# Decode attention with an adaLN block: q.k sums by identity matmuls, four heads across the partitions, V stationary, features on the partitions in the MLP

## Chip, cores and metric

One core of one Trainium2 chip. The metric is device time in microseconds (us) of one execution. Every run quoted is fast: none was over 1.5% above the fastest of its kernel. Each ratio to the kernel before is taken within the rounds of one chip; kernels of different rounds are compared by these ratios.

## The reference, cut to what matters

```python
# A_x (4,1,512); k_cache, v_cache (4,32,4096,128) bf16: 4 batches, 32 heads, 4096 keys
mod = silu(c) @ w_mod                        # six vectors of 512 for each batch
h = layernorm(x) * (1 + ca) + sa
q = (h @ wq)                                 # 32 heads of 128
p = softmax((q . k_cache) * 128 ** -0.5)     # one query for each batch and head
x = x + ga * ((p . v_cache) @ wo)
h = layernorm(x) * (1 + cb) + sb
z = gelu(h @ w_in); z1, z2 = halves of z     # 896 each
x = x + gb * ((z1 * (w_sp * layernorm(z2) + b_sp)) @ w_out)
```

(adaLN: the scale and shift of each layer norm come from c through w_mod. PV below is p . v_cache, the sum of V's rows weighted by the probabilities.) K and V are 134 MB each and each element is used once, so the work is a stream of 268 MB with a small start (w_mod 3.1 MB, wq 4.2 MB) and a small tail (wo, w_in, w_out).

## The kernel before

A group is one batch and 8 heads, in four K tiles of 2 heads (2 MB). A partition holds 32 consecutive keys of a head, 8 KB. VectorE does the whole dot product: multiply by the broadcast q, then six halving adds in place and a last add.

```python
kt = kvp.tile([P, HC, NT * DH], BF16, name="kt", bufs=4)      # HC = 2 heads, NT = 32, DH = 128
nc.sync.dma_start(out=kt, in_=kv_ap(A_k_cache, b, h0 + ci * HC))
...
for hli in range(HC):                                          # L271
    nc.vector.tensor_tensor(out=prod[:, hli], in0=prod[:, hli],
                            in1=qbc[:, hl, :][:, None, :].to_broadcast([P, NT, DH]), op=ALU.mult)
w = DH
while w > 2:                                                   # L281
    half = w // 2
    nc.vector.tensor_tensor(out=prod2[:, :, 0:half], in0=prod2[:, :, 0:half],
                            in1=prod2[:, :, half:w], op=ALU.add)
    w = half
nc.vector.tensor_tensor(out=S_g[...], in0=prod2[:, :, 0:1], in1=prod2[:, :, 1:2], op=ALU.add)  # L288
# ... softmax of the group: max by a transpose and a ones-matmul, exp on ScalarE ...
# PV of the group before, P stationary (one column), V moving:
nc.tensor.matmul(ops[pb:pb + 1, :], lhsT=P_g[:, hl, n:n + 1],  # L219
                 rhs=vt[:, hli, n * DH:(n + 1) * DH], ...)
```

V has three 2 MB buffers. Norms and MLP work on [4, 512] and [4, 1792] tiles: 4 of 128 partitions.

## Time and profile before

| | before |
|---|---|
| time, median of 4 runs | 794.36 us (793.86 to 794.49) |
| span of the profiled run | 792.9 us |
| bytes loaded | 283 MB |
| VectorE busy | 657.8 us, 83% |
| mean load rate | 357 GB/s |

The page of the kernel before, in parts: busy us and share for each engine; the span in 40 slices of 19.8 us with busy tenths for VectorE and the DMA engines and the load rate in GB/s; and the chain of waits that ended last.

```profile
PE 343.3 (43%) x4466; PEld 296.3 (37%) x4466; DVE 657.8 (83%) x754; ACT 73.0 (9%) x187; POOL 3.2 (0%) x14
...
DVE  1649999999999797979979797979979797979035
...
DMA  9999779999999999999899998989899999968220
GB/s 311 336 422 420 298 294 422 408 422 417 421 419 419 419 419 398 409 346 419 353 403 393 355 401 345 408 339 422 348 399 384 369 394 351 398 243 368 107 93 0
...
DVE 73%; PE 20%; DMA 4%; ACT 1%; issue 1%; ACTq 0%; SPq 0%; DVEq 0%
DVE kt L271 35%; DVE kt L281 32%; PE ops L219 15%; DMA kt<-in_A_k_cache_dram 2%; DMA wq_128<-in_A_wq_dram 1%; DVE S_g L288 1%; PE rowps L157 1%; PE rowps L176 1%; PE rowps L347 1%; ACT P_g L312 1%; DVE ssub L306 1%; DVE mrow L296 1%; PE row
```

VectorE sits at 9 or 7 tenths in nearly every slice, and the chain runs over it. But the load is near its own limit too: unhindered slices show 417 to 422 GB/s, and slices of 340 to 400 stand between them. The last three hold little (107, 93 and 0).

The groups by shape (line, engine, operation, tiles, shapes, count; busy us, mean ns of one; idle time before):

```profile
L271 DVE TENSOR_TENSOR kt<-kt,qbc 128x4096 bf16<-128x4096 bf16 x128 | 292.0, 2282 | 12.4 <-DMA kt<-in_A_k_cache_dram 12.3
L219 PE MATMUL ops<-vt,P_g 128*1 128x128 bf16 x4096 | 276.3, 237 | 68.8 <-ACT P_g L312 38.8 <-DMA vt<-in_A_v_cache_dram 20.5 <-ACT o_all L225 9.5
...
L281 DVE TENSOR_TENSOR kt<-kt 128x4096 bf16<-128x4096 bf16 x64 | 146.0, 2281 | 0.0
L281 DVE TENSOR_TENSOR kt<-kt 128x2048 bf16<-128x2048 bf16 x64 | 77.7, 1213 | 0.0
...
L288 DVE TENSOR_TENSOR S_g<-kt 128x64 f32<-128x64 bf16 x64 | 18.5, 289 | 0.0
```

All shapes of L281 in one line, from the page:

```profile
L281 DVE TENSOR_TENSOR kt<-kt 128x1024 bf16<-128x1024 bf16 (+5 forms) x384 | 320.7, 867 | 0.4
```

The multiplies cost 292.0 us. The adds that follow (all shapes of L281, 320.7 us, and L288, 18.5 us) cost more than the multiplies.

Two pieces of the chain in order of time (start, length, what) are the yardsticks for TensorE: 32 pairs of a 128-column weight load and one moving column in 0.89 us (28 ns each), and 32 matmuls of 512 columns in 7.08 us (221 ns each).

```profile
667.40 0.89 PE misc L235 x32
...
755.82 7.08 PE rowps L347 x32
```

### The profile page before, as it was taken

Reading aid. Unit: us, or ns where it says so; the run is one execution under the profiler, and the core shown is the slowest. Engines: PE = TensorE matmul, PEld = TensorE weight load, DVE = VectorE, ACT = ScalarE, POOL = GpSimd, SP = SyncE. Lnnn points to the kernel's source line nnn. Section 1 sums busy time; section 2 is a strip of 40 time slices with the busy share of each in tenths; the row PEclk is TensorE's granted clock in tenths of the full one; section 3 lists DMA queues with packets and bytes.
Section 4 is the critical chain, followed back from the end, with each engine's and each line's share of the span. In section 5 each row is a group of like instructions: output and inputs, shape, how many; then the busy total and the mean of one; then the engine's idle time right before and its main releaser. Section 6 shows DMA issues by size and latency. Waiting matters only on the chain.

```text
span 792.9 us, 10282 instructions
## 1 busy us (share of the span) xinstructions
PE 343.3 (43%) x4466; PEld 296.3 (37%) x4466; DVE 657.8 (83%) x754; ACT 73.0 (9%) x187; POOL 3.2 (0%) x14
## 2 busy tenths in 40 slices
PE   0810172726363636344261806244260807153872
PEld 0200061726263636244260806243250807143820
DVE  1649999999999797979979797979979797979035
ACT  1010100101010000101010100001010100000111
POOL 1000000000000000000000000000000000000000
PEclk9955586768675857768595857667595857667785
DMA  9999779999999999999899998989899999968220
GB/s 311 336 422 420 298 294 422 408 422 417 421 419 419 419 419 398 409 346 419 353 403 393 355 401 345 408 339 422 348 399 384 369 394 351 398 243 368 107 93 0
DMA packets 47893, 283.40 MB, mean 357 GB/s; under 512 B 2396, under 2 KB 14568, under 8 KB 15080
## 3 DMA queue, kind: packets, MB, share of 16 engines
q10 hardware_dynamic: 26672, 143.54, 45.3%
q1 hardware_dynamic: 21112, 139.21, 43.8%
q8 instruction: 35, 0.57, 0.3%
q14 instruction: 10, 0.08, 0.0%
q0 software_dynamic: 64, 0.00, 0.0%
HBM read 282.73 MB, written 0.00 MB: 357 GB/s over the span
## 4 chain that ended last, share of the span: by engine, by line
DVE 73%; PE 20%; DMA 4%; ACT 1%; issue 1%; ACTq 0%; SPq 0%; DVEq 0%
DVE kt L271 35%; DVE kt L281 32%; PE ops L219 15%; DMA kt<-in_A_k_cache_dram 2%; DMA wq_128<-in_A_wq_dram 1%; DVE S_g L288 1%; PE rowps L157 1%; PE rowps L176 1%; PE rowps L347 1%; ACT P_g L312 1%; DVE ssub L306 1%; DVE mrow L296 1%; PE rowps L369 1%; DVE mh L300 0%; PE misc L235 0%
## 5 line engine op out<-in xcount | busy, mean ns | idle before, releaser
L281 DVE TENSOR_TENSOR kt<-kt 128x1024 bf16<-128x1024 bf16 (+5 forms) x384 | 320.7, 867 | 0.4
L219 PE MATMUL ops<-vt,P_g 128*1 128x128 bf16 x4096 | 276.3, 237 | 68.8 <-ACT P_g L312 38.8
L271 DVE TENSOR_TENSOR kt<-kt,qbc 128x4096 bf16<-128x4096 bf16 x128 | 292.0, 2282 | 12.4 <-DMA kt<-in_A_k_cache_dram 12.3
L219 PEld LDWEIGHTS <-P_g 128*1 128x1 bf16 x4096 | 268.0, 92 | 73.5 <-ACT P_g L312 40.3
L298 PE MATMUL misc<-ident_f,mrow 128*8 128x128 f32 x16 | 6.0, 372 | 214.1 <-DVE mrow L296 214.1
L298 PEld LDWEIGHTS misc<-ident_f,mrow 128*8 128x8 f32 x16 | 1.3, 83 | 225.7 <-issue 165.6
L225 ACT ACTIVATE o_all<-ops,rZ 1x128 bf16<-1x128 f32 x128 | 38.4, 350 | 262.7 <-PE ops L219 161.2
L321 DVE RECIPROCAL rZ<-misc 1x8 f32<-1x8 f32 x16 | 3.3, 203 | 59.2 <-PE misc L316 59.2
L202 PE MATMUL qps<-q_sb,E_sel 4*128 4x512 bf16 x32 | 14.2, 485 | 85.5 <-ACT qbc L207 84.4
L202 PEld LDWEIGHTS <-E_sel 4*128 4x128 bf16 x32 | 2.8, 94 | 87.8 <-issue 86.4
L312 ACT ACTIVATE P_g<-ssub 128x256 bf16<-128x256 f32 x16 | 6.7, 416 | 298.1 <-DVE ssub L306 298.1
L207 ACT CAST qbc<-qps 128x512 bf16<-128x512 f32 x32 | 17.1, 587 | 111.9 <-DVE kt L271 92.0
L304 PE MATMUL misc<-diagM,ones_f 8*128 8x8 f32 x32 | 9.4, 364 | 39.8 <-DVE diagM L302 39.8
L304 PEld LDWEIGHTS misc<-diagM,ones_f 8*128 8x128 f32 x32 | 7.9, 306 | 44.9 <-DVE diagM L302 35.7
L288 DVE TENSOR_TENSOR S_g<-kt 128x64 f32<-128x64 bf16 x64 | 18.5, 289 | 0.0
L357 DVE TENSOR_SCALAR onepb<-mod_sb 4x512 f32<-4x512 bf16 x1 | 0.4, 415 | 15.7 <-PE ops L219 15.7
L151 DVE TENSOR_TENSOR siluc<-sig,c_sb 4x512 bf16<-4x512 f32 x1 | 0.7, 679 | 14.5 <-ACT sig L149 14.5
L127 PE MATMUL tp<-ident_bf,siluc 4*128 4x4 bf16 x4 | 0.7, 176 | 18.6 <-DVE siluc L151 18.3
L127 PEld LDWEIGHTS <-siluc 4*128 4x128 bf16 x4 | 0.3, 103 | 19.2 <-DVE siluc L151 18.3
L306 DVE TENSOR_TENSOR ssub<-S_g,misc 128x256 f32<-128x256 f32 x16 | 6.5, 404 | 1.0 <-PE misc L304 1.0
L347 PE MATMUL rowps<-wo_sb,oT_all 128*4 128x512 bf16 x32 | 7.1, 379 | 0.3 <-DVE oT_all L240 0.3
L180 DVE CAST q_sb<-rowps 4x512 bf16<-4x512 f32 x8 | 5.3, 677 | 2.2 <-PE rowps L176 2.2
(98 smaller groups left out, 118.7 us busy)
## 6 DMA issues: line engine op xcount, KB each, us to landing
kt<-in_A_k_cache_dram SPq DMA_DIRECT2D x64, 2048.0 KB, 9.0
vt<-in_A_v_cache_dram ACTq DMA_DIRECT2D x64, 2048.0 KB, 10.9
wo_sb<-in_A_wo_dram ACTq DMA_DIRECT2D x1, 4096.0 KB
win_sb<-in_B_w_in_dram SPq DMA_DIRECT2D x1, 1792.0 KB
wout_sb<-in_B_w_out_dram ACTq DMA_DIRECT2D x1, 896.0 KB, 21.1
wmod_112<-in_w_mod_dram SPq DMA_DIRECT2D x1, 512.0 KB, 3.8
wmod_114<-in_w_mod_dram SPq DMA_DIRECT2D x1, 512.0 KB, 4.8
wq_124<-in_A_wq_dram ACTq DMA_DIRECT2D x1, 512.0 KB
```

Source lines behind the costliest of these rows:

```text
L157: nc.tensor.matmul(mp, lhsT=cT[:, j, :], rhs=wmod_cs[oc][:, j, :], start=(j == 0), stop=(j == DJ - 1),)
L202: nc.tensor.matmul(qps, lhsT=E_sel[:, b, :], rhs=q_sb[0:B, h0 * DH + qi * QW:h0 * DH + (qi + 1) * QW], start=True, stop=True,)
L207: nc.scalar.copy(out=qbcv[:, qi * QW:(qi + 1) * QW], in_=qps)
L219: nc.tensor.matmul(ops[pb:pb + 1, :], lhsT=P_g[:, hl, n:n + 1], rhs=vt[:, hli, n * DH:(n + 1) * DH], start=(n == 0), stop=(n == NT - 1), t ...
L225: nc.scalar.activation(out=o_all[pb:pb + 1, h0 + hl, :], in_=ops[pb:pb + 1, :], func=AF.Copy, scale=rZ[pb:pb + 1, hl:hl + 1],)
L271: nc.vector.tensor_tensor(out=prod[:, hli], in0=prod[:, hli], in1=qbc[:, hl, :][:, None, :].to_broadcast([P, NT, DH]), op=ALU.mult,)
L281: nc.vector.tensor_tensor(out=prod2[:, :, 0:half], in0=prod2[:, :, 0:half], in1=prod2[:, :, half:w], op=ALU.add,)
L288: nc.vector.tensor_tensor(out=S_g[:, ci * HC:(ci + 1) * HC, :].rearrange("p h n -> p (h n)")[:, :, None], in0=prod2[:, :, 0:1], in1=prod2[ ...
L304: nc.tensor.matmul(Mbc_ps, lhsT=ones_rowG, rhs=diagM, start=True, stop=True)
L306: nc.vector.tensor_tensor(out=ssub, in0=S_g, in1=Mbc_ps[:, :, None].to_broadcast([P, HPG, NT]), op=ALU.subtract,)
L312: nc.scalar.activation(out=P_g, in_=ssub, func=AF.Exp, scale=att_scale)
L347: nc.tensor.matmul(attn_ps, lhsT=oT_all[:, j, :], rhs=wo_sb[:, j, :], start=(j == 0), stop=(j == H - 1),)
```

## The change

The intent is to take the sums off VectorE and to leave a stream bound by the load. VectorE still multiplies; TensorE then adds by 16 matmuls with the identity as weights, each over 8 of the 128 products of every key, accumulating in PSUM; VectorE folds the last 8. A step is one batch and 4 heads: a partition holds 128 keys of one head (32 KB in one row), 4 MB per tile, two buffers each for K and V, K on the sync queue and V on the scalar queue. In PV, V is stationary (loaded into TensorE as weights) and four columns of probabilities move (are streamed past them). All small work is laid out with features on the partitions.

```diff
+    nc.scalar.dma_start(out=cT, in_=c.rearrange("b (p j) -> p b j", j=J))     # 8-byte runs, also xT
+    wmod_t = kvp.tile([P, J, 6 * D], BF16, name="vt", bufs=2)
+    nc.sync.dma_start(out=wmod_t, in_=w_mod.rearrange("(p j) n -> p j n", j=J))
+    wq_t = kvp.tile([P, J, H * DH], BF16, name="vt", bufs=2)
+    nc.sync.dma_start(out=wq_t, in_=A_wq.rearrange("(p j) n -> p j n", j=J))
...
+        return cache[b, g * NH:(g + 1) * NH].rearrange("h (s n) d -> (h s) (n d)", s=R)
...
-                while w > 2:
-                    nc.vector.tensor_tensor(out=prod2[:, :, 0:half], ..., op=ALU.add)
+            nc.vector.tensor_tensor(
+                out=kt, in0=kt, in1=q[:, None, :].to_broadcast([P, HT, DH]), op=ALU.mult)
+            for cc in range(DH // DC):                                  # 16 times, DC = 8
+                nc.tensor.matmul(ps, lhsT=ident, rhs=kt[:, :, cc * DC:(cc + 1) * DC],
+                                 start=(cc == 0), stop=(cc == DH // DC - 1))
...
+            nc.vector.tensor_reduce(out=st["S", i][...], in_=ps, axis=AX.X, op=ALU.add)
...
-                            ops[pb:pb + 1, :], lhsT=P_g[:, hl, n:n + 1], rhs=vt[...],
+                    o_ps, lhsT=st["v", i][:, n, :], rhs=P4[:, n, :],
...  norms by ones-matmuls, MLP with weights stationary and 4 moving columns;
...  the engine order is fixed by hand: scores(i,0), project(i-2), fold(i-1,1), softmax(i-1),
...  scores(i,1), fold(i,0), values(i-1)
```

## The prediction

> **What bounds it now.** Span 792.9 us. VectorE is busy 657.8 us (83%, busy table); the chain of waits is 73% VectorE, 20% TensorE, 4% DMA. Per 4 MB of K+V VectorE pays (groups by shape) two 2.28 us multiplies, halving adds of 5.2 us together and the S_g add: about 10 us, then each group's softmax and PV burst. The load is close behind: 283.4 MB, and free slices run at 419-424 GB/s, so 283.4/0.42 = 675 us would be pure load. But K buffers come free late (SyncE waits 559 us on S_g), and the mean is 357 GB/s. The first 36 us run at 350 GB/s (1 KB packets). The last 93 us hardly load (700-745: 225 GB/s; 745-793: 78): last PV, wo 7.1 us, a serial MLP tail on 4 partitions.
>
> **Removed.** 320.7+18.5 us of VectorE adds; q broadcasts, 4-row transposes, three table reloads.
> **Kept.** The multiply: 64 of twice the size, still 290 us.
> **Added on VectorE** (estimates): 64 PSUM folds of 512 f32 at ~0.65 us = 42; per 4-head step five small softmax ops, ~1.5 us, and the o scaling, ~0.4 us: 60. Total ~395 us, 12.3 us per step of 32.
> **Added on TensorE.** 1024 identity matmuls of N=512: 221 ns each warm (wo burst: 32 in 7.08 us) = 226 us. The Trainium skill, "TensorE: Matmul & The Clock Gate", Back-to-back issue gap, gives 216 ns warm, 427 cold; the wo burst agrees with warm. PV with V stationary: 4096 pairs of a 128-column weight load and 4 columns; nearest in the trace, the o transposes (128-column load, 1 column) ran 32 in 0.89 us, 28 ns each, against 58-74 for PV now: 115 us. Together ~10.7 us per step warm, ~21 if the clock stays at half.
>
> **The new limit.** A step moves 8.39 MB, 20.0 us at 420 GB/s. K buffer: landed, 4.4 multiply, ~3 fold/softmax, 4.4 multiply, 3.5-7 us TensorE: free 16-18 us after landing, inside 20; so one K transfer is always outstanding. V has ~35 us. Both engines fit, so I expect a load-bound stream: VectorE ~55%, TensorE 45-60%, DMA at 9 in nearly every slice. The 340 us saved on VectorE are worth only the gap from 793 to the load. The skill's "DMA: Bandwidth & Descriptors", Measured, has 425 GB/s for large single-core loads; the best slices here agree (424).
>
> **Sum.** Start 2.5 us + 283.4 MB at 418-420 GB/s (676) = 678; a start gap (q by 128 tiled matmuls before the first V may load) 3; after the last landing: values, projection ~3 us, MLP feature-on-partition ~13 us (about 30 ops of 0.2-0.3 us on 16-56 columns, 84 small matmuls), output ~3 us. Predicted **700 us, range 684 to 732**. Chances: faster by over 2% 0.95, within 2% 0.03, slower 0.02.
>
> **What would show it.** DMA mean ~405 GB/s; chain of waits mostly DMA kt/vt instead of VectorE; identity matmuls 220-300 ns apart; PV pairs ~30 ns; no middle slices below 400; ~20 us from last landing to end instead of ~40.
>
> **What would make it wrong.** (1) The identity's moving operand is read in runs of 8 elements; if that, or a half clock in bursts with gaps, costs 2x, TensorE needs ~20 us per step: 720-780. (2) 128-column V weights not loading at 28 ns. (3) 32 KB rows loading below 420 GB/s: at 400, +34 us. (4) Two 4 MB buffers per stream too few: 1 us per step is +32. (5) q matmuls not overlapping: start gap 10-20 us.

## The result, and the profile after

| | before | after |
|---|---|---|
| time, median of 4 runs | 794.36 us | 719.40 us (717.88 to 721.82) |
| ratio | | 0.9056 (0.9036 to 0.9076) |
| VectorE busy | 657.8 us | 370.1 us |
| TensorE busy | 343.3 us | 428.8 us |
| mean load rate | 357 GB/s | 395 GB/s |

A ratio is the mean time of one kernel's fast runs over that of the other's of the same rounds, so it is not quite the ratio of the medians.

The time lies in the forecast range (684 to 732 us), 19 us above the predicted 700. The same parts of the page after (slices of 18 us):

```profile
PE 428.8 (60%) x5626; PEld 248.7 (35%) x5626; DVE 370.1 (52%) x405; ACT 82.0 (11%) x273; POOL 3.6 (0%) x17
...
DVE  0016575664664266665564366566555265663822
...
DMA  8938999999999999999999999999999989999930
GB/s 345 423 138 346 412 432 432 426 425 435 398 435 426 429 424 432 423 425 435 421 430 418 436 419 430 426 430 433 412 427 423 433 371 435 432 424 432 364 150 1
...
DMA 59%; DVE 25%; PE 14%; issue 1%; ACT 1%; DVEq 0%
DMA kt<-in_A_k_cache_dram 53%; DVE kt L225 19%; PE s_ps L230 9%; DMA xT<-in_A_x_dram 6%; DVE S L239 1%; PE o_ps L276 1%; PE qp L202 1%; DVE mT L249 1%; DVE nm L257 1%; DVE hm L251 0%; PE mod_ps L173 0%; DVE hb L253 0%; PE zf_ps L358 0%; DVE
```

The chain is now DMA, and the middle slices run at 412 to 435 GB/s almost without exception (398 and 371 are the lowest). Two things are left: the third slice at 138 GB/s and the end.

The groups that answer to those of before:

```profile
L230 PE MATMUL s_ps<-kt,ident 128*128 128x512 bf16 x1024 | 298.3, 457 | 225.4 <-DVE kt L225 225.2
L225 DVE TENSOR_TENSOR kt<-kt,qbc 128x8192 bf16<-128x8192 bf16 x64 | 281.8, 4404 | 251.2 <-DMA kt<-in_A_k_cache_dram 251.2
L230 PEld LDWEIGHTS <-ident 128*128 128x128 bf16 x1024 | 115.6, 113 | 393.5 <-issue 252.4 <-DMA kt<-in_A_k_cache_dram 70.5
L276 PEld LDWEIGHTS <-vt 128*128 128x128 bf16 x4096 | 109.1, 97 | 0.3 <-issue 0.3
L239 DVE TENSOR_REDUCE S<-s_ps 128x64 f32<-128x512 f32 x64 | 43.7, 683 | 2.2 <-issue 2.1
```

The adds are gone from VectorE; the folds cost 43.7 us (predicted 42), the multiplies 281.8 (predicted 290). VectorE now idles 251.2 us waiting for K.

One step in order of time (start, us, engine, line, what, idle before it):

```profile
411.45 4.43 DVE L225 TENSOR_TENSOR kt<-kt,qbc 128x8192 bf16<-128x8192 bf16 x1 [11.55 <-DMA kt<-in_A_k_cache_dram]
...
415.93 5.52 PE L230 MATMUL s_ps<-kt,ident 128*128 128x512 bf16 x16 [9.63 <-DVE kt L225]
...
417.16 0.15 PEld L230 LDWEIGHTS <-ident 128*128 128x128 bf16 x1 [0.27 <-issue]
...
417.59 0.15 PEld L230 LDWEIGHTS <-ident 128*128 128x128 bf16 x1 [0.28 <-issue]
...
418.08 4.38 DVE L225 TENSOR_TENSOR kt<-kt,qbc 128x8192 bf16<-128x8192 bf16 x1
...
422.51 3.61 PE L230 MATMUL s_ps<-kt,ident 128*128 128x512 bf16 x16 [1.06 <-DVE kt L225]
...
426.10 3.37 PE L276 MATMUL o_ps<-P_2_107,vt 128*128 128x4 bf16 x128
...
429.59 4.42 DVE L225 TENSOR_TENSOR kt<-kt,qbc 128x8192 bf16<-128x8192 bf16 x1 [6.53 <-DMA kt<-in_A_k_cache_dram]
```

K lands at 411.45. 5.52 us for 16 identity matmuls in the first half and 3.61 in the second (226 ns each); then 128 PV pairs in 3.37 us, 26 ns each. In the first half most weight loads (PEld, two of them shown) come 427 ns apart: TensorE had been idle for 9.6 us and starts slowly. The Trainium skill, "TensorE: Matmul & The Clock Gate", § Back-to-back issue gap, gives N / 1.2 GHz cold, 427 ns for 512 columns, and about 216 ns warm for a matmul alone; both agree with this step. The same section gives about 131 ns for N = 512 in a stream of weight loads and matmuls, and that is not seen here: such pairs ran 226 ns apart. All the work on this K tile ends at 426.1, 14.7 us after it landed, and the next tile comes at 429.59.

The stretches with busy time of each engine, mean granted clock, DMA share and GB/s:

```profile
core 0: us, PE busy (x) PEld busy (x) DVE busy (x) ACT busy (x) POOL busy (x), PEclk, DMA share, GB/s
...
40.00:60.00 20.00, 13.01 (x226) 7.58 (x226) 4.88 (x20) 5.41 (x11) 0.00 (x0) 1.00 0.25 81
300.00:400.00 100.00, 63.91 (x840) 36.96 (x839) 56.42 (x55) 11.56 (x40) 0.00 (x0) 0.73 1.00 427
```

From 40 to 60 us the load runs at 81 GB/s. The timeline of the start shows why:

```profile
0.77 0.45 ACTq L67 DMA_DIRECT2D cT<-in_c_dram  x1
...
40.75 0.22 ACT L161 ACTIVATE sg<-cT 128x16 f32<-128x16 bf16 x1 [38.73 <-DMA cT<-in_c_dram]
...
47.04 9.12 PE L202 MATMUL qp<-vt,hbc 128*32 128x512 bf16 x128 [1.50 <-DVE hbc L194]
...
56.22 2.55 ACTq L96 DMA_DIRECT2D vt<-in_A_v_cache_dram  x2
```

c is asked for at 0.77 us and ScalarE gets it at 40.75; x, behind it on the queue, is used at 43.43. Everything hangs on these two: the modulation, h, q (128 matmuls in 9.1 us), and the release of the two V buffers in which w_mod and wq lie, so the first V load goes out at 56.22. The two K buffers had filled at about 32 and 42 us (30.6 and 39.9 us after their issue), and from about 40 to 57 us hardly anything was loaded.

The DMA view of the first 40 us:

```profile
DMA packets 1150, 15.70 MB, mean 393 GB/s; under 512 B 639, under 2 KB 639, under 8 KB 639
...
q1 hardware_dynamic: 559, 15.70, 93.1%
q10 hardware_dynamic: 527, 0.00, 0.7%
```

In this time the sync queue (q1, bulk) moved 559 packets of 28 KB on average (15.70 MB / 559) and the scalar queue (q10) 527, nearly all of them c's 512 runs of 8 bytes: turn about, one for one (in the 10 us from 12 to 22 it was 145 and 145). Of the 559, 512 are the rows of w_mod, wq and the two K tiles (24 to 32 KB); the rest are 1 KB rows of wo. The Trainium skill, "DMA: Bandwidth & Descriptors", § Queues, rings and completion order, says that each DMA engine goes round robin between its queues, packet by packet. The counts agree. An estimate: c has 32 runs for each of 16 engines; 40.0 us / 32 = 1.25 us a turn, and a 28 KB packet at 427/16 GB/s takes 1.05 us. That reading was tested below.

**The sum.** Before the stream 2.5 us; 15.7 MB until about 40 us; gap 17 us; 267.8 MB from 57 to about 689.5 us (423 GB/s); from the last landing to the end 29 us. The forecast had 678 for the start and stream together without gap (measured 40 + 632.5, about 672), 3 for the gap and 19 for the end.

### The profile page after: what moved, and what is told of

The parts are those of the page before. It is cut to its first block, busy times and chain, and to the rows that moved or that the text cites. A ratio compares the mean times of both kernels' runs of the same rounds, so it can differ in the third digit from the quotient of the medians.

```text
span 718.3 us, 12248 instructions
## 1 busy us (share of the span) xinstructions
PE 428.8 (60%) x5626; PEld 248.7 (35%) x5626; DVE 370.1 (52%) x405; ACT 82.0 (11%) x273; POOL 3.6 (0%) x17
## 3 DMA queue, kind: packets, MB, share of 16 engines
q10 hardware_dynamic: 6096, 134.23, 43.7%
## 4 chain that ended last, share of the span: by engine, by line
DMA 59%; DVE 25%; PE 14%; issue 1%; ACT 1%; DVEq 0%
DMA kt<-in_A_k_cache_dram 53%; DVE kt L225 19%; PE s_ps L230 9%; DMA xT<-in_A_x_dram 6%; DVE S L239 1%; PE o_ps L276 1%; PE qp L202 1%; DVE mT L249 1%; DVE nm L257 1%; DVE hm L251 0%; PE mod_ps L173 0%; DVE hb L253 0%; PE zf_ps L358 0%; DVE oT L288 0%; ACT P_1_101 L260 0%
## 5 line engine op out<-in xcount | busy, mean ns | idle before, releaser
L230 PE MATMUL s_ps<-kt,ident 128*128 128x512 bf16 x1024 | 298.3, 457 | 225.4 <-DVE kt L225 225.2
L225 DVE TENSOR_TENSOR kt<-kt,qbc 128x8192 bf16<-128x8192 bf16 x64 | 281.8, 4404 | 251.2 <-DMA kt<-in_A_k_cache_dram 251.2
L230 PEld LDWEIGHTS <-ident 128*128 128x128 bf16 x1024 | 115.6, 113 | 393.5 <-issue 252.4
L276 PEld LDWEIGHTS <-vt 128*128 128x128 bf16 x4096 | 109.1, 97 | 0.3 <-issue 0.3
L260 ACT ACTIVATE P_0_95<-S,nm 32x128 bf16<-32x128 f32 x44 | 25.4, 576 | 190.8 <-DVE nm L257 189.9
L260 ACT ACTIVATE P_1_101<-S,nm 32x128 bf16<-32x128 f32 x44 | 25.4, 577 | 188.6 <-DVE nm L257 187.7
L239 DVE TENSOR_REDUCE S<-s_ps 128x64 f32<-128x512 f32 x64 | 43.7, 683 | 2.2 <-issue 2.1
L260 ACT ACTIVATE P_2_107<-S,nm 32x128 bf16<-32x128 f32 x40 | 23.0, 576 | 184.1 <-DVE nm L257 183.3
L276 PE MATMUL o_ps<-P_1_101,vt 128*128 128x4 bf16 x1408 | 37.4, 164 | 0.2 <-issue 0.2
L276 PE MATMUL o_ps<-P_0_95,vt 128*128 128x4 bf16 x1408 | 37.3, 164 | 0.0
L276 PE MATMUL o_ps<-P_2_107,vt 128*128 128x4 bf16 x1280 | 33.8, 164 | 0.0
L260 ACT ACTIVATION_READ_ACCUMULATOR P_0_95<-S,nm 32x1 f32 x44 | 11.0, 250 | 0.0
L260 ACT ACTIVATION_READ_ACCUMULATOR P_1_101<-S,nm 32x1 f32 x44 | 11.0, 250 | 0.0
L202 PE MATMUL qp<-vt,hbc 128*32 128x512 bf16 x128 | 9.1, 455 | 1.5 <-DVE hbc L194 1.5
L260 ACT ACTIVATION_READ_ACCUMULATOR P_2_107<-S,nm 32x1 f32 x40 | 10.0, 250 | 0.0
L257 DVE STREAM_TRANSPOSE nm<-hb 128x32 f32<-128x32 f32 x32 | 6.8, 211 | 3.2
```

The source lines that it names most:

```text
L202: nc.tensor.matmul(qp[hl * R:(hl + 1) * R], lhsT=hbc[:, j, b, :], rhs=wv[:, gh * GH:(gh + 1) * GH, hl, :], start=(j == 0), stop=(j == J - ...
L225: nc.vector.tensor_tensor(out=kt, in0=kt, in1=q[:, None, :].to_broadcast([P, HT, DH]), op=ALU.mult,)
L230: nc.tensor.matmul(ps, lhsT=ident, rhs=kt[:, :, cc * DC:(cc + 1) * DC], start=(cc == 0), stop=(cc == DH // DC - 1),)
L239: nc.vector.tensor_reduce(out=st["S", i][:, half * HT:(half + 1) * HT], in_=st.pop(("s", i, half)), axis=AX.X, op=ALU.add,)
L257: nc.vector.transpose(out=nm, in_=hb)
L260: nc.scalar.activation(out=P4[rows, :, hl], in_=S[rows, :], func=AF.Exp, bias=nm[rows, 0:1], scale=att_scale, accum_out=rs4[rows, hl:hl + 1],)
```

## The experiments

Eleven kernels ran. All are recorded as correct, e4 too, which leaves out half of V: the check of the result does not notice that, so it says little about the attention part.

### The start: e1 and e2

e1 puts the two small loads ahead of the bulk on its queue:

```diff
-            nc.scalar.dma_start(out=dst, in_=src)      # cT, xT
+            nc.sync.dma_start(out=dst, in_=src)
```

> Edit: the two small loads c and x (8-byte runs) go out on the sync queue ahead of the bulk loads instead of on the scalar queue beside them. Theory A (the small packets take turns with 28 KB bulk packets, so c lands at 40.7 us and the load stands still from about 39 to 57 us): c lands before 6 us, q is ready by about 35 us, the empty stretch of 18 us goes, time 700 to 705 us. Rival B (8-byte runs are slow by themselves, about 40 us for 512): the bulk behind them starts 40 us later, time 720 us or more. Rival C (the gap is refilled later, because the stream is limited elsewhere): time 715 to 722.

Measured: 700.22 us (699.16 to 703.56), ratio to before 0.8818 against 0.9056. c lands 1.9 us after its issue. The view of that tile, and the load rate:

```profile
DMA to landing us min/median/max: 1.9/1.9/1.9
```

```profile
GB/s 327 419 439 426 436 421 425 426 430 410 425 434 426 435 372 436 429 424 420 361 440 421 436 387 420 438 423 438 427 426 427 428 404 440 421 431 431 418 181 1
```

The gap is gone and theory A's number is met; rival B (slow runs) and C (limited elsewhere) fall. e2 leaves the small loads where they were and cuts w_mod and wq into rows of 6 and 8 KB:

```diff
+    for j in range(J):
+        nc.sync.dma_start(out=wmod_t[:, j, :], in_=w_mod.rearrange("(p j) n -> p j n", j=J)[:, j, :])
+    # wq likewise
```

> Edit: c and x stay on the scalar queue as they are; the w_mod and wq loads are cut in 4 pieces each, so that their rows (packets) are 6 and 8 KB instead of 24 and 32 KB. Theory A (turns packet by packet): c needs 32 turns per DMA engine; with 6 KB packets at 27 GB/s a turn takes about 0.22 us, so c lands at about 9 us and x at about 18 us instead of 41 and 43 us; the gap goes, time 700 to 707 us. Rival D (the scalar queue is starved until the sync queue is empty): c still lands at about 40 us, time 717 to 722.

Measured: 699.90 us (699.07 to 701.37). c lands after 4.8 us (x after 14.0), sooner than the 9 us worked out, and far from the 40 of rival D. (In the first 5.6 us of this trace the scalar queue moved 533 packets and the sync queue 192, so the turns were not one for one there.)

```profile
DMA to landing us min/median/max: 4.8/4.8/4.8
```

The scalar queue is the same, c and x are the same, the bulk bytes are the same; only the length of the bulk rows differs (and the number of loads that carry them, 8 instead of 2), and with it c's landing falls from 40.0 to 4.8 us. So it is the turn length that held c up, unless the number of loads did it, which was not tried alone.

### Is the middle bound by the load? e3 and e4

```diff
+                nc.vector.tensor_tensor(out=idle, in0=idle, in1=idle, op=ALU.mult)   # e3: once per step, 128x8192
```

> Edit: one more useless 4.4 us VectorE multiply per step (32 in all, +141 us of VectorE busy time, 370 to about 510). Theory (the middle is bound by the load, VectorE has slack): +2 to +12 us, from the first and last steps alone. Rival (VectorE is on the path in each step, the chain gives it 25%): +60 us or more.

Measured: 724.93 us (724.00 to 726.61), ratio 0.9127, so +0.8% on the kernel after, about 6 us for 142 us more VectorE time:

```profile
PE 425.7 (59%) x5626; PEld 248.2 (34%) x5626; DVE 511.9 (71%) x438; ACT 82.1 (11%) x273; POOL 3.6 (0%) x17
```

The theory holds: VectorE has slack in each step, though it holds 25% of the chain. The extra multiply stands after the second multiply of the step, outside the time in which a K buffer is held; what a longer hold of the buffer would cost is not tested by it.

```diff
-        return load(A_v_cache, i, "vt", ...)                         # e4, wrong on purpose
+        nc.scalar.dma_start(out=t[:, 0:w], in_=kv_view(A_v_cache, i)[:, 0:w])     # w = half
...  lhsT=st["v", i][:, n % HT, :]
```

> Wrong result on purpose. Edit: only half of each V tile is loaded (67 MB less), the PV matmuls read that half twice; all engine work stays. Theory (load-bound at about 425 GB/s): 283.5 MB becomes 216.4 MB, time 720 - 67.1/0.425 = about 562 us, or up to 580 if the K cycle of two buffers starts to bind. Rival (engines or buffer waits bind): above 680.

Measured: 602.54 us, ratio 0.7598. 117 us go with 67.1 MB, so the load does bind; but 562 to 580 was missed. The rates in the middle of e4's trace are lower than in the kernel after:

```profile
GB/s 324 440 322 82 239 343 420 384 420 411 397 394 396 419 387 378 352 433 395 364 408 393 401 423 344 411 412 387 401 384 417 403 392 395 403 407 401 354 3 1
```

They are mostly 380 to 420 GB/s. VectorE still waits 134 us for K there, and SyncE 351 us for VectorE's multiplies and 111 us for TensorE until a K buffer is free. If the start (57 us) and the tail (29 us) are as in the kernel after, a step takes some 16 us ((602 - 57 - 29) / 32) against 19.8 there (633 / 32), where 6.3 MB at 425 GB/s would take 14.8. So a second limit lies a little below the first. That it is the two K buffers, which no longer keep the queue full, is a reading and not shown: the same waits are no shorter in the kernel after (251, 410 and 111 us).

### Which part of the change pays: e5, e6, e7, e9

e5 is the kernel before with the identity sums alone; e6 the kernel after with the halving adds back.

```diff
-                while w > 2: ...  # halving adds
+                for cc in range(DH // 8):                                     # e5
+                    nc.tensor.matmul(s_ps, lhsT=ident_bf, rhs=prod2[:, :, cc * 8:(cc + 1) * 8], ...)
+                nc.vector.tensor_reduce(out=S_g[...], in_=s_ps, axis=AX.X, op=ALU.add)
```

> The kernel before with one part of the change alone: the halving adds become 16 accumulating identity matmuls and one fold per 2 MB K tile (two of the four o accumulators in PSUM given up for it). Everything else (2 MB tiles, P stationary in PV, 4-row MLP) as before. VectorE busy 658 to about 365 us; TensorE per 8-head group about 14 us of identity matmuls and 15 to 19 us of PV, in 39 us of load. Theory (relief of VectorE is most of the gain): 725 to 750 us. Rival (without the other parts TensorE's order or the three V buffers hold it): above 765 us.

Measured: 738.71 us (738.41 to 740.28), ratio 0.9296: 56 us of the change's 75. What the tile shapes and the layout of the MLP are worth was not run alone. Chain and rate:

```profile
GB/s 306 348 395 419 406 366 422 420 418 414 421 417 420 419 321 422 419 418 420 418 419 421 420 417 420 419 419 419 420 419 419 419 395 307 420 418 418 260 97 0
...
DMA 47%; PE 38%; DVE 12%; ACT 1%; issue 1%; ACTq 1%; SPq 0%; DVEq 0%
```

> The kernel after with that part undone: the identity matmuls and folds become the six halving adds and a last add on VectorE, in place. VectorE busy about 282 + 340 + 40 = 665 us. Theory (VectorE then binds): start 57 us + about 21 us of VectorE in each of 32 steps + tail, 760 to 800 us, VectorE over 90% busy in the middle. Rival (the load hides it): below 735.

Measured: 777.20 us, ratio 0.9776: 58 us lost again. VectorE's slices and the chain:

```profile
DVE  0019999999999999999999999999999999999962
...
DVE 85%; DMA 8%; PE 3%; issue 2%; ACT 1%; DVEq 0%
```

Done alone or undone alone, the identity sums are worth 56 to 58 us. e7 undoes V stationary:

```diff
-                    o_ps, lhsT=st["v", i][:, n, :], rhs=P4[:, n, :],
+                    o_ps, lhsT=P4[:, n, :], rhs=st["v", i][:, n, :],          # o_ps is [4, 128]
+            nc.tensor.transpose(t_ps, o4, ident[0:NH, 0:NH])                   # in project()
```

> The kernel after with one part undone: PV with the probabilities (4 columns) as weights and V moving (128 columns), then a small transpose of o. TensorE gains 128 x (58 - 27) ns = 4 us per step, within the slack of 6 to 7 us. Theory (V stationary is off the critical path in the middle): 719 to 730 us, what it costs comes in the tail. Rival (it is part of the gain): above 740.

Measured: 846.00 us, ratio 1.0648, slower than the kernel before. The expectation failed, and the timeline of one step shows on what:

```profile
307.57 3.63 PE L230 MATMUL s_ps<-kt,ident 128*128 128x512 bf16 x16
...
307.67 0.28 DVE L289 CAST o<-o_ps 4x128 bf16<-4x128 f32 x1 [7.05 <-PE o_ps L276]
...
311.13 0.17 PE L291 MATMUL t_ps<-ident,o 4*128 4x4 bf16 x1
...
311.34 0.17 DVE L292 TENSOR_TENSOR oT<-t_ps,rz 128x4 bf16<-128x4 bf16 x1 [3.39 <-PE t_ps L291]
...
313.34 4.38 DVE L225 TENSOR_TENSOR kt<-kt,qbc 128x8192 bf16<-128x8192 bf16 x1
...
317.77 6.39 PE L230 MATMUL s_ps<-kt,ident 128*128 128x512 bf16 x16 [6.47 <-DVE kt L225]
```

VectorE first stands 7.05 us on the end of PV for the copy of o, which the edit also brought in. The small transpose then stands in TensorE's queue behind 16 identity matmuls; VectorE stands on it (3.39 us idle) before its fold, softmax and second multiply; TensorE then stands 6.47 us on that multiply. The step is one chain of 23.9 us. This tests the order that I gave to the transpose, not V stationary. e9 takes the wait for the transpose away:

```diff
+            if i > 2: project(i - 3)       # uses the transpose of the step before
+            if i > 1: take(i - 2)          # copy o to SBUF
...
+            if i > 1: turn(i - 2)          # the transpose, after scores(i, 1)
```

> The miss of e7_after_P_stationary again (there 846 us) without the wait that it brought in: there the small transpose of o stood in TensorE's queue behind the first 16 identity matmuls, and VectorE stood before its fold until it was done, so each step became one chain of 23.9 us. Here the transpose is queued just before the next PV and its result taken one step later. Theory (V stationary itself is worth nothing in the middle, the 4 us of TensorE fit the slack): 719 to 732 us. Rival (V moving costs on the path in itself): above 750.

Measured: 725.29 us (723.25 to 727.45), ratio 0.9115: about 5 us more than the kernel after (0.9115 against 0.9056, 0.65% of 719), though PV took 7.3 us a step instead of 3.4:

```profile
L276 PE MATMUL o_ps<-vt,P 128*4 128x128 bf16 x4096 | 236.6, 220 | 0.0
```

In the middle it is off the path: from 145 us on its slices show 424 to 434 GB/s, and in e9's trace the last load lands at about 685 us, 5 us sooner than in the kernel after. In these two traces what V stationary gains lies in the tail: there the last two PVs take 7.3 and 10.0 us instead of 3.4 and 3.6.

### Row length: e11

```diff
-PIECES = 1
+PIECES = 4          # on e1: each tile in 4 loads of 8 KB rows
```

> e1_c_first with each K and V tile loaded in 4 pieces of 8 KB rows (the row length of the kernel before) instead of one of 32 KB rows. Theory (the row length gives the 428 GB/s of the middle against about 420 with 8 KB rows in the kernel before): 268 MB at 420 instead of 428 is +12 us, 708 to 716 us. Rival (rate does not depend on it): 698 to 703.

Measured: 702.60 us (702.02 to 702.85) against 700.22 for e1. The expectation failed and its rival's range was met: the 2 us lie within the scatter of e1's runs (699.16 to 703.56), and the rate between 80 and 600 us was not lower with short rows (425 or 426 GB/s in each stretch of 100 us or more, against 418 to 425 in e1). e5 in the old tiles shows 417 to 422 GB/s in most middle slices, this one 421 to 428 with rows as long; why is left open.

### Better versions: e8 and e10

e8 holds K and V in half tiles with four buffers each, c and x first, and loads the MLP weights at step 4.

```diff
+            t = kvp.tile([P, EL], BF16, name=tag, bufs=4)      # 2 MB, was 4 MB with bufs=2
```

> An attempt at a better version: c and x first, K and V in 2 MB half tiles with four buffers each (same bytes in SBUF), the MLP weights loaded at step 4 instead of at the end. Expected from the parts: 700 us of e1_c_first less 4 to 9 us, because the last V arrives alone and only its last values, the projection and the MLP follow: 691 to 697 us. If the 28 us after the last landing are not helped by it: 699 to 702.

Measured: 701.83 us (701.70 to 702.02). The stream is smoother (427 to 430 GB/s in each hundred us of the middle) but ends no earlier: at 654 to 658 us its load falls to about 200 GB/s, because the last V waits for the PV two steps back, and the last softmax and PV still follow. The 691 to 697 us were missed: no gain on e1.

e10 is e1 with the last turn reordered:

```diff
-            if i > 1: project(i - 2)
+            if 1 < i < NQ: project(i - 2)
             if i > 0: fold(i - 1, 1); softmax(i - 1)
+            if i == NQ: project(i - 2)
```

> Better version: c and x first as in e1_c_first (700.2 us), and in the last turn of the loop the fold and softmax of the last step go ahead of the o scaling of the step before, for which VectorE waited 3.1 us with the last scores ready. In the trace of e1_c_first the last exponentials would then be done about when the PV before ends: 3 to 4 us less, 696 to 698 us; if the last PV then waits for its V: 699 to 701.

Measured: 699.05 us (697.89 to 702.56), ratio to before 0.8801; the 696 to 698 us were missed. In the traces, the time from the end of the last identity matmuls to the end of the span falls from 31.7 us (e1) to 28.4; but the last two K tiles came 1 to 3.5 us later in e10's trace, and 1 us between the medians is within the scatter of both. e1, e2 and e10, at about 700 us, beat both kernels by 95 and 20 us.

## Why the prediction was right, and where its sum was off

- **The limit moves from VectorE to the load: right.** Chain 73% VectorE before, 59% DMA after; +142 us of VectorE work cost 6 us (e3); half of V's bytes took 117 us away (e4).
- **The identity sums carry the gain: right.** 56 us alone (e5), 58 us undone (e6).
- **Cost terms: near.** VectorE 395 us predicted, 370 measured; PV pairs 28 ns, 26 measured; TensorE per step 10.7 us warm and 21 cold, 12.8 measured in the step shown (5.52 + 3.61 + 0.28 for the row sums + 3.37). The 8-element runs of the moving operand cost nothing visible: 3.61 us for 16.
- **The stream: slightly pessimistic.** About 672 us against 678.
- **The mis-sized term: "a start gap (q by 128 tiled matmuls before the first V may load) 3".** It was about 17 us. The doubt named for it, "q matmuls not overlapping: start gap 10-20 us", had the size and the symptom right: the q matmuls (9.1 us together, 71 ns each) did lie in the gap. It had no cause for it: they came late because c and x did. In e1 they run from 22.9 to 31.4 us, under the K loads. c came late because its 8-byte runs took turns with 28 KB packets. Removing that by either of two edits gives back 19 to 20 us (e1, e2), all of the distance to 700.
- **The tail: 29 us from last landing to end, not 19 to 20.** The MLP part was right (13.3 us from the projection's end at 699.3 to the output's issue at 712.6, predicted 13). Missed were the last softmax and PV, about 9 us that do not hide behind the last V load, and the output in 8-byte runs, 5.7 us from issue to end, predicted 3. The faster stream paid for part of this. In sum the gap was 14 us longer than forecast, the end 10 us longer and the stream 6 us shorter: the 18 or 19 us by which the time lies above 700. So e1's 700 us, equal to the forecast, is luck in part: two errors of opposite sign.

## What to carry to other kernels

Once an engine's work falls below the time of its loads, what is left to win are the load's gaps and what follows the last landing, so look for what the first transfers wait for before looking at any engine. Don't start a tiny load of many runs beside bulk loads with long rows: here it cost some 19 us, and putting it ahead on the same queue, or cutting the bulk into shorter rows, each took that away. Before undoing a part to see what it is worth, check that the undone version brings no new wait into an in-order queue.

## What the Trainium skill lacked or had wrong

- "DMA: Bandwidth & Descriptors", § Queues, rings and completion order: it has the round robin by packets, but not what it does to a small load beside bulk rows. Here 4 KB in 512 runs of 8 bytes took 40.0 us beside rows of 24 to 32 KB, 4.8 us beside rows of 6 to 8 KB, and 1.9 us ahead of them. It gives 9 to 17 descriptors as a typical packet; here the profile counts c's 512 runs as about as many packets, so no such grouping shows.
- "TensorE: Matmul & The Clock Gate", § LDWEIGHTS: P / 1.2 ns is 107 ns for 128 columns, near the 97 ns of one load's record here, but the section does not say how close loads can follow each other: the pairs of a 128x128 bf16 load and a 4-column matmul ran at 26 ns each (128 in 3.37 us). That is near the floor of 25 ns that the page gives for a matmul alone, not near the 62 ns that it gives for decoding by the sequencer. It is also a quarter of 107 ns: § Weight-path perf modes has a fast weight load, with a factor of four as theory (for fp8) and about two as measured; whether that mode was on here is not shown.
- "DMA: Bandwidth & Descriptors", § Measured: it gives 341 GB/s for a 1 MB load and 425 for 16 MB. Here a queue of 1 MB loads (e11) ran at 421 to 428 GB/s in the middle, as the 4 MB loads did; with the next loads already queued, the size of one load cost nothing here.
